# A planner's assumed distance from TensorE to its readers, its booking of indirect transfers, and its due times are changed

## The chip, the cores and the metric

The kernel runs on one core of one Trainium2 chip. The metric is the device time of one execution in microseconds; runs are compared by their median.

## The reference

Two parts, one after the other. The first is a causal convolution of 8 sequences of 5696 steps with 128 channels by a filter as long as the sequence, written with Fourier transforms. The second sends each of the 8 x 5696 = 45,568 rows of 128 numbers to one of eight experts.

```python
Yf = np.fft.rfft(x, n=2*S, axis=1) * np.fft.rfft(h, n=2*S, axis=0)[None]
x  = np.fft.irfft(Yf, n=2*S, axis=1)[:, :S, :].reshape(N, D)
logits = x @ w_gate + modality_bias[modality_id]
e_idx  = np.argmax(logits, axis=1)
gate_w = softmax(logits)[np.arange(N), e_idx]
for e in range(E):                                    # E = 8, F = 1024
    out[e_idx == e] = gate_w * (np.maximum(x @ w1[e], 0) @ w2[e])
```

## The kernel before, in words

All data are 32-bit floats. Where TensorE has to keep full precision at its fast rate, an operand is split into a high and a low part, and three products (high by high, low by high, high by low) stand for one. ScalarE makes the high part, VectorE or GpSimd the low one.

The eight sequences are worked in four groups of two (g = 0 to 3). For each group there are three passes: **first** (`stage1`, line 300, 45 columns in 23 pairs), which writes `z` to memory; **over** (`stage23`, 64 rows, lines 584 to 616), which multiplies by the filter's transform, transforms back in part and writes `u`; and **route** (`stage4`, 23 pairs in chunks of four), which ends the transform (line 700 or 706), turns the rows (line 718), makes the gate logits (line 725), ranks them on VectorE (lines 758 to 800), and sends each block of 128 rows to its expert's region with one indirect transfer on GpSimd's queue (line 814). A full chunk has 16 of these.

The experts' tiles follow: 81 of 512 rows and 23 of 256 in five **levels** of 14, 22, 22, 23 and 23. Level g needs the routed rows of groups 0 to g; the last two need all of them. A tile is loaded on SP's queue (line 895), with weights (line 902), turned (line 921), and then runs eight times: first product (lines 935 to 937), ReLU and high part on ScalarE (line 940), low part on VectorE (line 943), second product (lines 951 to 953). The result is copied, turned (line 960), weighted (line 963) and scattered with four indirect transfers (line 967).

Past the first pass of group 0 the order of each engine's instructions comes from `Plan`, an event simulation in Python that runs when the kernel is built. A step has a duration for each engine that may do it, steps that it waits for, buffers that it takes and gives back, and a due time. Whenever an engine is free in the simulation, it takes the ready step with the earliest due time. That order is all that is kept: on the chip each engine works through its list in that order and waits on semaphores; no planned time is executed. `SYNC` is the time that the plan leaves between the end of a step and the start of a step on another engine that reads it. `RATE` and `LAND` describe the one transfer channel of the plan: a load or store occupies it for its bytes by `RATE` and is there `LAND` later. Indirect transfers (steps with `lag`) don't occupy that channel; they are only kept to four in 5.6 us, or 6.8 us once the tiles' first due time is past. `AIMS` holds the due times at which each pass of each group and each level of tiles begins and ends; a pass's steps are spread evenly between them.

Buffers that tie the order: seven PSUM banks shared by all passes, three first products in flight (`ph_sl`), four pairs of `hh` and `hl`, six `t` buffers, one transfer list on SP.

Of the kernel before, what the change touches and what calls it, by code (L numbers as in the profile page):

```python
# [45 lines left out]
RTB = 8  # L46

AIMS = {
    "first": (None, (-302, 250), (72, 321), (497, 681)),
    "over": ((-196, 106), (75, 320), (458, 614), (745, 1009)),  # L50
    "route": ((65, 348), (139, 704), (632, 1015), (984, 1478)),
    "weights": (341, 635),
    "tiles": (405, 700, 1107, 1532, 1617, 1651),
}
RUNS = (1, 2, 2, 2, 4)
WP = 256
# [42 lines left out]
class Plan:  # L99

    SYNC = {"PE": 0.22, "DVE": 0.15, "ACT": 0.15, "POOL": 0.2, "SP": 0.1, "-": 0.0}
    LAND = 2.6
    RATE = 0.31e6
    BURST = 4, 5.6, 6.8

    def __init__(self):
# [17 lines left out]
    def run(self):  # L126
        ready = {e: [] for e in self.SYNC}
        busy = {e: False for e in ready}
        total = {e: 0.0 for e in ready}
        events = []  # L130
        count = 0
        channel = woken = 0.0
        begun = [-100.0] * self.BURST[0]

        def push(t, kind, x):
            nonlocal count
            heapq.heappush(events, (t, count, kind, x))
            count += 1

        def enable(x):  # L140
            if x.early is not None and now < x.due - x.early:
                push(x.due - x.early, "enable", x)
                return
            for e in x.work:
                bisect.insort(ready[e], (x.due, x.n, x))

        def release(steps):
            for y in steps:
                y.left -= 1
                if not y.left:  # L150
                    enable(y)

        def reached(x, same):
            e = next(iter(x.work))
            release(y for y in x.next if (list(y.work) == [e]) == same)

        def first(e):
            nonlocal woken

            apart = begun[-self.BURST[0]] + self.BURST[1 if now < AIMS["tiles"][0] else 2]  # L160
            kept = now >= apart and any(r[2].lag for r in ready["POOL"])
            for r in ready[e]:
                x = r[2]

                main = next(iter(x.work))
                if main != e and not (busy[main] or main == "POOL" and kept) or e == "POOL" and kept and len(x.work) > 1:
                    continue
                if x.lag and now < apart:
                    if woken < apart:
                        woken = apart  # L170
                        push(apart, "wake", None)
                    continue
                if all(len(p.idle) >= sum(q is p for q, _ in x.take) for p, _ in x.take):
                    return x

        now, started = 0.0, 0
        for x in self.steps:
            if not x.left:
                enable(x)
        while True:  # L180
            for e in ready:
                x = None if busy[e] else first(e)
                if x is None:
                    continue
                x.start = now
                started += 1
                for p, key in x.take:
                    x.st[key] = p.take()
                for o in x.work:
                    ready[o].remove((x.due, x.n, x))  # L190
                x.emit(e)
                busy[e] = True
                total[e] += x.work[e]
                end = now + x.work[e]
                push(end, "idle", (e, x))
                if x.lag:
                    begun.append(now)
                if x.bytes:
                    channel = max(channel, end) + x.bytes / self.RATE
                    end = channel + self.LAND  # L200
                    push(end, "same", x)
                else:
                    push(end if len(x.work) == 1 else end + self.SYNC[e], "same", x)
                push(end + x.lag, "done", x)
                push(end + x.lag + self.SYNC[e], "next", x)
            if not events:
                break
            now = events[0][0]
            while events and events[0][0] <= now:
                _, _, kind, x = heapq.heappop(events)  # L210
                if kind == "idle":
                    busy[x[0]] = False
                    release(x[1].behind)
                elif kind == "done":
                    for p, key in x.free:
                        p.give(x.st[key])
                elif kind == "enable":
                    x.early = None
                    enable(x)
                elif kind != "wake":  # L220
                    reached(x, kind == "same")
        assert started == len(self.steps), "steps that wait for each other"
        self.total, self.end = total, now
# [924 lines left out]
```

## Time and profile before

| | |
|---|---|
| median of 3 runs | 2410.16 us (2404.16 to 2418.43) |
| the profiled execution | 2395.75 us |
| its span, first to last instruction | 2394.0 us |
| TensorE busy | 2126.2 us (89%) |
| VectorE, ScalarE, GpSimd busy | 68%, 54%, 52% |
| mean granted TensorE clock | 0.932 |

A share is an average over passes with different limits, so the stretches are read one by one. "Waited for" is idle time of an engine in front of an instruction that ended when the named instruction was done; "issue" and "remote" are such time that the trace puts down to no instruction of the core. A busy TensorE counts modelled ends of its matmuls.

### The profile page before, as it was taken

What the parts mean: (1) busy time and instruction counts of PE and PEld (TensorE: products, weight loads), DVE (VectorE), ACT (ScalarE), POOL (GpSimd) and SP (SyncE); (2) the same over time, 40 slices, a digit from 0 to 9 for tenths busy, and PEclk for the clock granted to TensorE, in tenths of its full rate; (3) what the DMA queues carried; (4) which work ended last, traced back from release to release, by engine and by line L of the source; (5) the groups of instructions that cost most, each with busy time, mean ns of one, the idle gap of its engine ahead of it and who ended that gap; (6) DMA issues with size and microseconds to landing.
All of it is one profiled execution on the core that took longest, in us unless ns stands there. A gap on an engine that the chain in (4) does not pass through costs nothing.

```text
span 2394.0 us, 39278 instructions
## 1 busy us (share of the span) xinstructions
PE 2126.2 (89%) x11514; PEld 1774.0 (74%) x11514; DVE 1633.3 (68%) x3107; ACT 1291.1 (54%) x2584; POOL 1251.1 (52%) x1278
## 2 busy tenths in 40 slices
PE   5699876987999999788999999879878999999997
PEld 4577776765788787676888787658666778888897
DVE  5499764887689999776688986446434745555554
ACT  5566664654656676654556555335433444444453
POOL 2178554785477777567366665452444333333332
PEclk8899876998999999889999999889989999999999
DMA  8999765998998898764455643333212151122630
GB/s 285 301 298 299 246 215 172 289 329 275 280 304 282 275 312 266 243 226 135 118 151 165 196 125 121 123 116 92 84 55 93 45 151 44 45 80 69 222 107 26
DMA packets 228265, 434.54 MB, mean 182 GB/s; under 512 B 35798, under 2 KB 94906, under 8 KB 224209
## 3 DMA queue, kind: packets, MB, share of 16 engines
q1 hardware_dynamic: 204448, 384.15, 51.3%
q0 software_dynamic: 23600, 47.88, 6.1%
q8 instruction: 91, 1.49, 0.3%
q14 instruction: 126, 1.02, 0.1%
HBM read 408.11 MB, written 175.95 MB: 244 GB/s over the span
## 4 chain that ended last, share of the span: by engine, by line
PE 43%; issue 6%; DVE 5%; another core or an unknown queue 3%; DMA 2%; ACT 1%; POOL 1%; SPq 0%; POOLq 0%; DVEq 0%; ACTq 0%
PE bank L937 5%; PE bank L952 5%; PE bank L935 5%; PE bank L951 5%; PE bank L936 5%; PE bank L953 5%; PE bank L706 2%; PE bank L584 2%; PE pl L725 1%; PE bank L960 1%; PE bank L921 1%; DVE hl L943 1%; DVE t L591 1%; POOL out L967 1%
## 5 line engine op out<-in xcount | busy, mean ns | idle before, releaser
L943 DVE SCALAR_TENSOR_TENSOR hl<-bank,hh 128x512 fp32r<-128x512 f32 x740 | 503.7, 688 | 394.2 <-ACT hh L940 318.3
L940 ACT ACTIVATE hh<-bank 128x512 fp32r<-128x512 f32 x740 | 439.0, 598 | 524.3 <-PE bank L937 382.2
L967 POOL DMA_INDIRECT out<-of,mrt x370 | 370.2, 1001 | 514.5 <-DVE of L963 391.2
L814 POOL DMA_INDIRECT rows<-rt,idx x360 | 376.5, 1046 | 126.6 <-issue 94.2
L951 PE MATMUL bank<-hh,slot 128*128 128x512 f32 (+1 forms) x744 | 311.0, 418 | 46.5 <-ACT hh L940 32.3
L952 PE MATMUL bank<-hl,slot 128*128 128x512 f32 (+1 forms) x744 | 294.0, 395 | 17.2 <-DVE hl L943 11.7
L935 PE MATMUL bank<-mxh,slot 128*128 128x512 f32 (+1 forms) x744 | 305.4, 410 | 3.0 <-DMA slot<-weights 2.2
L936 PE MATMUL bank<-mxl,slot 128*128 128x512 f32 (+1 forms) x744 | 289.3, 389 | 4.0 <-DVE mxl L927 3.9
L953 PE MATMUL bank<-hh,slot 128*128 128x512 f32 (+1 forms) x744 | 289.7, 389 | 0.0
L591 DVE TENSOR_TENSOR t<-bank,hs 96x512 f32<-96x512 f32 x415 | 263.1, 677 | 38.3 <-PE bank L584 20.5
L937 PE MATMUL bank<-mxh,slot 128*128 128x512 f32 (+1 forms) x744 | 288.5, 388 | 0.0
L584 PE MATMUL bank<-zb,m 96*96 96x256 f32 x896 | 233.6, 390 | 2.8 <-DMA zb<-z 1.6
L951 PEld LDWEIGHTS bank<-hh,slot 128*128 128x128 f32 x744 | 144.5, 194 | 79.5 <-ACT hh L940 41.1
L952 PEld LDWEIGHTS bank<-hl,slot 128*128 128x128 f32 x744 | 144.4, 194 | 53.3 <-DVE hl L943 23.8
L584 PEld LDWEIGHTS bank<-zb,m 96*96 96x96 f32 x896 | 146.1, 168 | 46.3 <-DMA zb<-z 2.3
L401 ACT COPY ut<-bank 90x512 f32<-90x512 f32 x189 | 109.6, 581 | 108.5 <-PE bank L616 48.3
L937 PEld LDWEIGHTS bank<-mxh,slot 128*128 128x128 f32 x744 | 143.7, 193 | 29.6
L935 PEld LDWEIGHTS bank<-mxh,slot 128*128 128x128 f32 x744 | 144.1, 194 | 29.1 <-DMA slot<-weights 2.7
L936 PEld LDWEIGHTS bank<-mxl,slot 128*128 128x128 f32 x744 | 144.4, 194 | 28.3 <-DVE mxl L927 5.6
L953 PEld LDWEIGHTS bank<-hh,slot 128*128 128x128 f32 x744 | 144.0, 194 | 27.2
L300 PE MATMUL bank<-xx,ft 128*128 128x256 f32 x810 | 128.2, 311 | 20.7 <-ACT ft L504 20.5
L692 POOL TENSOR_TENSOR uu<-uu 128x512 fp32r<-128x512 f32 x48 | 62.4, 1308 | 148.6 <-ACT uu L688 147.2
(222 smaller groups left out, 4423.7 us busy)
## 6 DMA issues: line engine op xcount, KB each, us to landing
slot<-weights SPq DMA_DIRECT2D x158, 1024.0 KB
z<-z SPq DMA_DIRECT2D x180, 256.0 KB
uu<-u SPq DMA_DIRECT2D x159, 256.0 KB
zb<-z SPq DMA_DIRECT2D x112, 360.0 KB
u<-ut SPq DMA_DIRECT2D x112, 360.0 KB
raw<-in_w SPq DMA_DIRECT2D x88, 256.0 KB
mrt<-rows SPq DMA_DIRECT2D x81, 260.0 KB
hs<-hd SPq DMA_DIRECT2D x96, 192.0 KB
```

Of the source, the lines that this page charges most:

```text
L584: nc.tensor.matmul(two(st["px"])[:KP, h], mm, both["zb"][:, k % 2, 1 - h], start=True, stop=True)
L591: nc.vector.tensor_tensor(st[f"t{h}"].rearrange("p j (b d) -> p j b d", d=D), px[:KP, h].rearrange("p (b d) -> p b d", d=D).unsqueeze(1).t ...
L814: nc.gpsimd.indirect_dma_start(views[count[0] % NVIEW], bass.IndirectOffsetOnAxis(ap=rs["idx"][:, t + c:t + c + 1], axis=0), st["rt"][:, c ...
L935: nc.tensor.matmul(po, w[0][:, fs], xh, start=True, stop=False)
L936: nc.tensor.matmul(po, w[0][:, fs], xl, start=False, stop=False)
L937: nc.tensor.matmul(po, w[1][:, fs], xh, start=False, stop=True)
L940: nc.scalar.activation(hf["hh"], hf["ph"], AF.Relu)
L943: nc.vector.scalar_tensor_tensor(hf["hl"], hf["ph"], 0.0, hf["hh"].bitcast(F32), op0=ALU.max, op1=ALU.subtract)
L951: nc.tensor.matmul(po, w[0][:, fs], hf["hh"][:, cs], start=k == 0, stop=False)
L952: nc.tensor.matmul(po, w[0][:, fs], hf["hl"][:, cs], start=False, stop=False)
L953: nc.tensor.matmul(po, w[1][:, fs], hf["hh"][:, cs], start=False, stop=k == 7)
L967: nc.gpsimd.indirect_dma_start(oviews[(t * NSUB + c) % NVIEW], bass.IndirectOffsetOnAxis(ap=st["rt"].bitcast(I32)[:, c, D + 1:D + 2], axis=0),
```

## The change

Four things, all in what the plan assumes; no instruction of the kernel is written differently.

- `SYNC["PE"]`, the distance from the end of a TensorE step to steps of other engines that read it, goes from 0.22 to 1.5 us.
- Each indirect transfer books 66e3 bytes on the plan's transfer channel.
- `RATE` goes from 0.31e6 to 0.30e6 bytes a microsecond.
- The due times of all passes and levels are other ones.

```diff
 AIMS = {
-    "first": (None, (-302, 250), (72, 321), (497, 681)),
-    "over": ((-196, 106), (75, 320), (458, 614), (745, 1009)),
-    "route": ((65, 348), (139, 704), (632, 1015), (984, 1478)),
-    "weights": (341, 635),
-    "tiles": (405, 700, 1107, 1532, 1617, 1651),
+    "first": (None, (-356, 245), (71, 322), (490, 734)),
+    "over": ((-251, 93), (112, 389), (452, 612), (756, 1007)),
+    "route": ((113, 343), (138, 685), (612, 1003), (965, 1563)),
+    "weights": (343, 669),
+    "tiles": (392, 685, 1115, 1550, 1570, 1652),
 }
...
-    SYNC = {"PE": 0.22, "DVE": 0.15, "ACT": 0.15, "POOL": 0.2, "SP": 0.1, "-": 0.0}
+    SYNC = {"PE": 1.5, "DVE": 0.15, "ACT": 0.15, "POOL": 0.2, "SP": 0.1, "-": 0.0}
     LAND = 2.6
-    RATE = 0.31e6
+    RATE = 0.30e6
+    ROWS = 66e3
...
                 if x.lag:
                     begun.append(now)
+                    channel = max(channel, now) + self.ROWS / self.RATE
                 if x.bytes:
                     channel = max(channel, end) + x.bytes / self.RATE
```

## Rows read from the trace of the kernel before

**Rows 1.** The head of the page: span, and each engine's busy time, share and instructions; and the part on transfer queues, the queue of GpSimd's indirect transfers (packets, MB, share of the 16 transfer engines).

```profile
span 2394.0 us, 39278 instructions
PE 2126.2 (89%) x11514; PEld 1774.0 (74%) x11514; DVE 1633.3 (68%) x3107; ACT 1291.1 (54%) x2584; POOL 1251.1 (52%) x1278
...
q0 software_dynamic: 23600, 47.88, 6.1%
```

**Rows 2.** Busy time by stretch: the stretch and its length, then busy us (instructions) of TensorE, its weight loads, VectorE, ScalarE, GpSimd, then granted TensorE clock, share of the transfer engines, GB/s.

```profile
112.00:270.00 158.00, 149.88 (x880) 123.40 (x879) 151.97 (x231) 105.92 (x208) 120.87 (x116) 0.98 0.90 286
270.00:420.00 150.00, 108.53 (x627) 99.68 (x626) 83.16 (x190) 84.07 (x194) 69.91 (x66) 0.72 0.65 205
420.00:600.00 180.00, 154.97 (x790) 120.25 (x789) 149.62 (x314) 94.22 (x203) 122.75 (x131) 0.90 0.94 297
600.00:960.00 360.00, 341.09 (x1947) 284.57 (x1947) 318.59 (x565) 240.60 (x519) 248.28 (x250) 1.00 0.91 286
960.00:1140.00 180.00, 149.57 (x790) 123.88 (x788) 123.19 (x273) 102.83 (x215) 113.71 (x111) 0.89 0.63 199
...
1440.00:1960.00 520.00, 441.16 (x2104) 352.57 (x2103) 263.98 (x619) 224.58 (x438) 230.18 (x235) 0.90 0.32 97
1960.00:2394.00 434.00, 417.84 (x2469) 364.94 (x2468) 234.53 (x366) 203.65 (x365) 136.96 (x141) 0.99 0.26 87
```

**Rows 3.** TensorE's waits from 270 to 420 us, longest in total first: who waited for whom, us in total, times, longest.

```profile
PE bank L718 <- DVE rt L403: 16.0, 6, 11.9
PE pl L725 <- issue: 8.0, 4, 6.1
PE bank L718 <- issue: 6.8, 3, 3.2
PE bank L300 <- ACT ft L504: 5.6, 2, 2.8
...
```

**Rows 4.** The same from 420 to 600 us.

```profile
PE bank L610 <- issue: 6.2, 1, 6.2
PE bank L610 <- POOL t L598: 5.8, 8, 1.6
PE bank L610 <- DVE t L598: 3.0, 2, 2.8
...
```

**Rows 5.** The same from 960 to 1140 us.

```profile
PE bank L300 <- ACT ft L504: 10.8, 1, 10.8
PE bank L951 <- ACT hh L940: 9.9, 4, 3.8
PE bank L952 <- DVE hl L943: 3.2, 4, 2.4
PE bank L706 <- POOL uu L692: 3.1, 1, 3.1
...
```

**Rows 6.** The same from 1440 to 1960 us.

```profile
PE bank L951 <- ACT hh L940: 21.2, 7, 10.3
PE bank L951 <- issue: 13.9, 6, 6.6
PE bank L960 <- ACT ot L401: 10.1, 5, 4.2
PE pl L725 <- DVE yt L403: 6.1, 3, 3.4
PE bank L706 <- DVE hl L943: 5.1, 1, 5.1
PE bank L960 <- issue: 5.0, 2, 4.0
PE pl L768 <- DVE oh L763: 4.7, 2, 2.7
PE bank L936 <- DVE mxl L927: 3.9, 2, 3.7
PE bank L952 <- DVE of L963: 3.1, 1, 3.1
...
```

**Rows 7.** Instructions in order of time, three steps of a tile in the last stretch: start, duration, engine, line, operation, and in brackets the engine's idle time before it and what ended it.

```profile
2002.64 0.39 PE L937 MATMUL bank<-mxh,slot 128*128 128x512 f32 x1
2003.07 0.60 ACT L940 ACTIVATE hh<-bank 128x512 fp32r<-128x512 f32 x1 [0.80 <-PE bank L937]
2003.69 0.69 DVE L943 SCALAR_TENSOR_TENSOR hl<-bank,hh 128x512 fp32r<-128x512 f32 x1 [0.71 <-ACT hh L940]
```

**Rows 8.** Instructions in order of time around 1600 us: the first and the last of GpSimd's 20 transfers that follow one another there, then ScalarE's and SP's next instructions.

```profile
1587.49 1.00 POOL L814 DMA_INDIRECT rows<-rt,idx  x1 [2.11 <-DVE rt L800]
...
1611.81 0.97 POOL L967 DMA_INDIRECT out<-of,mrt  x1 [0.30 <-issue]
1615.73 1.08 ACT L940 ACTIVATE hh<-bank 128x512 fp32r<-128x512 f32 x2 [13.33 <-remote]
1615.73 0.08 SPq L902 DMA_DIRECT2D slot<-weights  x1
```

**Rows 9.** Instructions in order of time at the end of the last route pass: its last logits, the first transfer of its last chunk, and the first load of a tile of the fourth level.

```profile
1860.28 0.51 PE L725 MATMUL pl<-wg,yt 128*128 128x8 f32 x4
1910.22 0.99 POOL L814 DMA_INDIRECT rows<-rt,idx  x1 [7.98 <-DVE rt L800]
1948.09 0.36 SPq L895 DMA_DIRECT2D mrt<-rows  x1
```

## The prediction, made before the changed kernel ran

> **What bounds the kernel now.** I read the head of the page first: TensorE is busy 2126 of 2394 us, no other engine above 68% [rows 1]. So the question is where TensorE is not kept busy. Busy time by stretch answers it [rows 2]. From 112 to 270 us and from 600 to 960 us VectorE is the fuller engine or nearly so (152 of 158, 319 of 360 us) and TensorE misses only 8 and 19 us. From 1960 us to the end only tiles are left; TensorE misses 16 of 434 us and has its clock. The loss lies in four stretches: 270 to 420 (108.5 of 150 us busy, granted clock 0.72), 420 to 600 (155 of 180, 0.90), 960 to 1140 (150 of 180, 0.89) and 1440 to 1960 (441 of 520, 0.90). In the first, third and last of them no engine is full, so there the order of the lists sets the pace.
>
> TensorE's waits in these stretches say what it stands behind [rows 3 to 6]: nearly always a reader of its own results (rt, hh, hl, ot, yt, t) on ScalarE, VectorE or GpSimd, or time put down to nobody. A transfer is not among the long ones. The timeline of one of the longest shows a second thing [rows 8]: GpSimd issues 20 indirect transfers without a pause from 1587.5 to 1612.8 us, and ScalarE and SP both stand until 1615.73 us, 3 us after the last one ends; ScalarE had stood for 13.3 us, with TensorE's product done. A wait like this has no producer that could be ordered earlier.
>
> **The change, part by part.** Nothing is added or removed; the 39,278 instructions stay, but for low parts that the plan may hand from VectorE to GpSimd or back. What can change is each engine's order, SP's transfer list and GpSimd's included.
>
> *The distance, 0.22 to 1.5 us.* In the trace ScalarE starts 0.43 us after the last of three matmuls starts, and VectorE's part begins 0.62 us after that [rows 7]; 0.22 is therefore about the true distance, and 1.5 is slack, 1.28 us of it. Each reader of TensorE, and all that follows from it, TensorE's own next step included, is planned 1.28 us later, so some 1.28 us more of independent matmuls stand ahead of every matmul that needs a reader. A wait on a reader can shrink by at most 1.28 us. From the rows, taking min(longest, 1.28) for the longest of each row and at most 1.28 us for each of the others: [rows 3] 5.4 + 3.2 + 3.8 + 2.6 = 15.0 of 36.4 us; [rows 4] 1.3 + 5.8 + 1.5 = 8.6 of 15.0; [rows 5] 1.3 + 5.1 + 2.1 + 1.3 = 9.8 of 27.0; [rows 6] 9.0 + 7.7 + 6.4 + 3.8 + 1.3 + 2.3 + 2.6 + 1.5 + 1.3 = 35.9 of 73.1. The sum is 69 of 152 us. That is the upper bound by this part alone. The lower bound is nothing: at most three first products may be in flight, so in a burst like [rows 8] the extra work is used up at the first wait, and the later waits of the same burst end when GpSimd ends. I take half, 35 us, because in the last stretch the 7 waits of one row include one of 10.3 us and six that share 10.9 us [rows 6]: the short ones can go, the long ones can't. In the stretches where VectorE is full I take nothing; a deeper order can't speed VectorE.
>
> In the last stretch I take nothing either: its order already lets TensorE run (418 of 434 us).
>
> *The clock.* A stretch with waits has a granted clock of 0.72 to 0.90 and one without has 0.98 to 1.00 [rows 2]; that is a mixture of 1.2 and 2.4 GHz, and each wait that goes also gives some of it back. The Trainium skill, page "TensorE: Matmul & The Clock Gate", section "Why this matters for your kernels", says that idle gaps between bursts of matmuls put the clock back to its lower level; the trace agrees (0.72 where the waits are thickest). By it the gain would exceed the waits. I leave this gain out of the sum and let it stand against waits that arise anew.
>
> *The booking and the rate.* An indirect transfer moves 47.88 MB / 730 = 66 KB [rows 1], so the booking is true to size: 0.22 us of channel each, 160 us over the kernel, and every load behind it is planned that much later. Where transfers are dense (0.90 to 0.94 of the engines [rows 2]) work that reads a load then stands later in the lists of ScalarE and VectorE, which could only help; but TensorE shows no long wait on a load there. The lower end is nothing. The upper end is the one wait that ends with a load's conversion, 10.8 us at ft [rows 5], which the first term has already counted by 1.3. I take nothing.
>
> *The due times.* For most passes they move by under 40 us and keep their order. One pair moves against another: the last route pass (984 to 1478, now 965 to 1563) against the third level's tiles (1107 to 1532, now 1115 to 1550). Its last pair was due at 984 + 494 x 22/23 = 1456.5 and is now due at 1537. Tiles due behind it: (1532 - 1456.5)/19.3 = 3.9 before, (1550 - 1537)/19.8 = 0.7 now. These tiles hide the chain from the last logits to the fourth level. It took from 1860.3 to 1948.1 us [rows 9], 88 us, but 50 us of that pass before the last chunk's first transfer, which in the end waited for VectorE's line 800. Ranking is a few short instructions; if 40 of the 50 us can go, 48 are needed, and cover that shrinks by 3.2 tiles of 434/34.5 = 12.6 us (23 tiles and 23 half ones [rows 2]), 40 us, just about still hides it. The range of this part is 0 to +40 us; I take 0. On the other side the same work is spread over 598 instead of 494 us, so chunks of 16 transfers stand further apart; I count no gain for it, since a chunk's 16 still become ready together.
>
> Sum: 2395.75 us for the profiled execution, less 35, is 2361. That execution lay 14.4 us under the median of the runs (2410.16). On the scale of the median I predict **2375 us**; with one fifth to all of the bound, its own range is 2341 to 2396.
>
> **The rivals.**
>
> *The bursts decide, and the time stays.* TensorE's long waits end when GpSimd's run of transfers ends [rows 8], the 16 transfers of a chunk become ready at once in either plan, and the distance is no part of that. Then 2410, give or take 12. For it: of the 152 us, 83 lie beyond the 1.28. Against it: many short waits that are plainly readers, such as the eight at t of 5.8 us [rows 4].
>
> *A hole before the fourth level; slower.* The cover of the last route pass is gone and VectorE still makes the tables first. TensorE then stands 40 us at the change of level; the last stretch of gain is lost and of the other three half remains (17 us): 2395.75 - 17 + 40 + 14.4 = 2433. It decides if the last chunk's first transfer (line 814) starts less than about 38 us before the third level's last matmul (from its 1910.2 to the load at 1948.1 it was 38 us [rows 9]). For it, the arithmetic of the due times; against it, the slack that the chain has.
>
> *Buffers run short in the plan; slower.* A bank is held 1.28 us longer at every step: the plan counts 0.88 + 0.22 + 1.30 = 2.40 us for line 584 and its reader, then 3.68. If seven banks don't do, the plan starts steps late and the order in the full stretches has holes that the chip does not need. If VectorE in 600 to 960 us fell to its share of 420 to 600 (0.83 instead of 0.885), that stretch would take 23 us more, and with no gain elsewhere the time is 2433 too. The Trainium skill speaks for this rival: "PSUM — Partial Sum Buffer", section "Summary: rules for kernel authors", asks to empty PSUM promptly because it is tight. The rows before show no sign of it, but they are of the short distance.
>
> *The bursts break up; faster than forecast.* With readers later, more low parts wait for GpSimd between transfers, and a run of 20 falls into shorter ones. Then the rows' waits in 1440 to 1960 go (73) with the bounds of the other three (33): 2395.75 - 106 + 14.4 = 2304. For it, the wider route pass; against it, VectorE is half empty there (264 of 520 us [rows 2]), so it will keep most low parts.
>
> **How the numbers follow.** Forecast 0.46, no change 0.20, hole 0.14, short buffers 0.08, broken bursts 0.12. This kernel's runs spread over 0.6%, so 0.5%, 12 us, is about what can be told from no change. Faster by more: most of the forecast and the broken bursts, 0.57; within: 0.21; slower: 0.22. The range 2318 to 2431 leaves out about two thirds of the broken bursts and half of either slower case, 0.19 in all.
>
> **What would show it.** Right: fewer and shorter waits of lines 951, 960, 718 and 610 on their readers in the four stretches, with the waits of over 5 us still there at runs of 16 to 20 transfers; the last 434 us unchanged; the clock in the second stretch above 0.72. Wrong: a gap of TensorE over 10 us where the first tile of the fourth level is loaded (hole); VectorE's share from 600 to 960 us under 0.85 (buffers); no run of over 12 transfers past 1440 us (bursts broken); or gains in the stretches where VectorE is full, which I price at nothing.

## The result

| | before | after |
|---|---|---|
| median of 4 runs, us | 2407.16 (2397.46 to 2418.43) | 2291.59 (2286.97 to 2298.12) |
| profiled execution, us | 2395.75 | 2289.67 |
| its span, us, and mean granted clock | 2394.0, 0.932 | 2287.8, 0.953 |

The ratio of the medians is 0.952 (0.947 to 0.957). The kernel is 116 us faster; 35 were forecast, and 2291.59 lies under the range. The direction is right and the size is not. Lines of the kernel after stand two lower than those of before: 935 is now 937, 940 is 942, 960 is 962.

Four runs of those below took 680 to 2910 us longer than the others of their kernel; the ratios leave them out, the medians do not.

The head of the page after answers to [rows 1]. TensorE's modelled busy time fell by 50 us (2126 to 2076) and its idle time by 55 (211 to 156, counted from the instructions in order of time, from the first matmul past the first pass of group 0, at 111 and 108 us, to the last matmul).

```profile
span 2287.8 us, 39250 instructions
...
PE 2076.3 (91%) x11514; PEld 1751.0 (77%) x11514; DVE 1637.0 (72%) x3097; ACT 1276.0 (56%) x2579; POOL 1256.2 (55%) x1293
```

Busy time by stretch, kernel after, columns as in [rows 2]; the last stretch starts with its fourth level:

```profile
270.00:420.00 150.00, 114.81 (x717) 105.39 (x716) 98.71 (x216) 91.58 (x215) 86.83 (x85) 0.78 0.76 241
420.00:600.00 180.00, 148.82 (x744) 115.48 (x743) 144.05 (x286) 90.80 (x195) 118.57 (x131) 0.91 0.91 281
600.00:960.00 360.00, 346.88 (x2001) 294.48 (x1999) 320.49 (x602) 242.53 (x526) 254.60 (x253) 0.99 0.91 286
960.00:1140.00 180.00, 158.51 (x869) 133.21 (x870) 133.16 (x264) 103.20 (x221) 112.04 (x111) 0.94 0.63 199
...
1844.00:2287.00 443.00, 425.21 (x2494) 370.57 (x2492) 233.38 (x369) 205.46 (x369) 138.30 (x143) 0.99 0.27 87
```

Equal clock times are no longer equal work, so I compare where each level begins. The first products of the first four levels start at 599.6, 1075.6, 1546.09 and 1957.17 us before, and at 560.7, 1031.4, 1503.71 and 1843.99 us after; the fifth level follows the fourth. The kernel after is 39 us ahead at the first level, 44 at the second, 42 at the third and 113 at the fourth; what follows takes 437 us before and 444 after.

Even these places are not equal work. Counted in order of time, 2562, 5052, 7381 and 9034 matmuls stand ahead of the four levels before, and 2446, 4971, 7441 and 9021 after. The first level is 39 us earlier with 116 fewer matmuls ahead of it, so a part of the 39 is work put off. The idle time of TensorE has no such doubt: up to the first level, in each of the first three levels, and behind them it is 75, 38, 31, 64 and 4 us before, and 72, 30, 26, 23 and 6 after. So 41 of the 55 us went within the third level. That level's own stretch, first in the kernel before and then in the kernel after:

```profile
1546.09:1957.17 411.08, 347.52 (x1654) 278.02 (x1653) 204.77 (x466) 173.32 (x335) 180.43 (x184) 0.91 0.31 91
```

```profile
1503.71:1843.99 340.28, 317.21 (x1581) 258.73 (x1580) 198.15 (x448) 161.72 (x312) 179.44 (x185) 0.97 0.34 106
```

TensorE's waits there, kernel after, longest first; they answer to [rows 6]:

```profile
PE bank L962 <- ACT ot L403: 8.6, 4, 3.1
PE bank L953 <- issue: 6.4, 1, 6.4
PE bank L923 <- DMA mrt<-rows: 2.8, 1, 2.8
PE bank L953 <- ACT hh L942: 1.7, 2, 1.5
```

The wait of the second product on ScalarE's ReLU, 21.2 us with one of 10.3 in [rows 6], is 1.7 us, from 1440 us on too. Between 1440 and 1503.71 us one longer wait stands, 8.9 us at line 962, put to "issue". The 10.3 us wait was one that ends with GpSimd's run of transfers, the sort that I had said would stay; in the kernel before, in order of time, right behind ScalarE's row of [rows 8]:

```profile
1616.38 0.80 PE L951 MATMUL bank<-hh,slot 128*128 128x512 f32 x1 [10.32 <-ACT hh L940]
```

ScalarE's own waits tell the same. These are its longest rows put to "remote" over the whole execution, first in the kernel before, then in the kernel after; "remote" means here that the trace shows nothing on the core that ended them:

```profile
ACT hh L940 <- remote: 58.4, 15, 13.3
...
ACT gt L676 <- remote: 15.3, 1, 15.3
...
ACT ot L401 <- remote: 9.6, 3, 6.5
```

```profile
ACT ot L403 <- remote: 12.8, 2, 11.3
...
ACT yt L403 <- remote: 10.7, 2, 8.8
...
ACT hh L942 <- remote: 9.3, 4, 3.2
```

All such waits of ScalarE come to 103 us before and 56 after. Before, each of the 26 ends inside a run of eight or more transfers or less than 5 us behind one. VectorE has such waits too, 42 us before and 20 after. The longest wait of [rows 3], 11.9 us of line 718 for VectorE, was of this sort as well: in the kernel before, ScalarE and VectorE were released together, 2.6 us after a run of 20 transfers had ended at 392.86 us:

```profile
395.48 0.40 ACT L676 CAST gt<-gs 128x256 fp32r<-128x256 f32 x1 [15.34 <-remote]
395.53 0.69 DVE L403 COPY rt<-bank 128x512 f32<-128x512 f32 x1 [13.12 <-remote]
```

SP's list stands with them (kernel before, then after):

```profile
SPq L902 <- remote: 72.2, 6, 25.6
```

```profile
SPq L669 <- remote: 14.9, 3, 9.5
```

### The profile page after: what moved, and what is told of

Its sections match the earlier page's. It is cut to its first block, busy times and chain, and to the rows that moved or that the text cites. A ratio compares the mean times of both kernels' runs of the same rounds, so it can differ in the third digit from the quotient of the medians.

```text
span 2287.8 us, 39250 instructions
## 1 busy us (share of the span) xinstructions
PE 2076.3 (91%) x11514; PEld 1751.0 (77%) x11514; DVE 1637.0 (72%) x3097; ACT 1276.0 (56%) x2579; POOL 1256.2 (55%) x1293
## 5 line engine op out<-in xcount | busy, mean ns | idle before, releaser
L953 PE MATMUL bank<-hh,slot 128*128 128x512 f32 (+1 forms) x744 | 306.0, 411 | 9.6 <-issue 6.4
L954 PE MATMUL bank<-hl,slot 128*128 128x512 f32 (+1 forms) x744 | 287.1, 386 | 4.3 <-DVE hl L945 3.2
L955 PE MATMUL bank<-hh,slot 128*128 128x512 f32 (+1 forms) x744 | 285.3, 384 | 0.0
L599 POOL TENSOR_TENSOR t<-t,t 96x256 f32<-96x256 f32 x88 | 71.6, 813 | 140.3 <-DVE t L593 104.3
```

What stands on the lines that cost most here:

```text
L953: nc.tensor.matmul(po, w[0][:, fs], hf["hh"][:, cs], start=k == 0, stop=False)
L954: nc.tensor.matmul(po, w[0][:, fs], hf["hl"][:, cs], start=False, stop=False)
L955: nc.tensor.matmul(po, w[1][:, fs], hf["hh"][:, cs], start=False, stop=k == 7)
```

## The experiments

My theory after the result had two parts. The distance removes waits on readers, as forecast, and it also shortens what ScalarE and SP stand while GpSimd's transfers run without a pause [rows 8]. The first rival: the new due times and the booking do the second part, by spreading the chunks. The second rival: the standing has no price, and all of the gain is order.

A fact for reading what follows: the runs are of several chips, and the chips are of two kinds. On chips 0 and 5 and on the one of the result above, whose number is not known, the kernel before takes 2391 to 2407 us. On chips 8, 12 and 7 it takes 2232 to 2233 us, and in no trace taken there is a wait of ScalarE or VectorE put to "remote". I call the first kind **standing**, because there engines stand in runs of transfers, and the second **quiet**. The unaltered kernel before was timed on the quiet chips but not traced there. Each numbered chip was used for one set of runs, so whether a chip keeps its kind is not shown. Each ratio is against the kernel before on the same chip.

### The parts, on a quiet chip (chip 8, before 2232.38 us)

*The distance alone:*

```diff
-    SYNC = {"PE": 0.22, ...
+    SYNC = {"PE": 1.5, ...
```

> The kernel before with one part of the change: the distance from TensorE to its readers 1.5 instead of 0.22 us; due times, rate and booking as before. If the distance is what gained (theory one: short waits on readers go, and with them the lower clock), most of the 116 us come with it: 2300 to 2345 us. If the due times are what gained (theory two: the last route pass is spread wider and the runs of transfers fall apart), this stays within 2395 to 2425. If the parts only work together (theory three: due times are set for one plan and are wrong for another), it is 2360 to 2450, without a side.

2212.58 us, 0.991 (0.987 to 0.995).

*The due times alone:*

```diff
-    "first": (None, (-302, 250), (72, 321), (497, 681)),
...
+    "tiles": (392, 685, 1115, 1550, 1570, 1652),
```

> The kernel before with the new due times alone; distance 0.22, rate and booking as before. Theory one (distance): 2390 to 2425. Theory two (due times): 2300 to 2345, with no run of over 12 transfers past 1440 us. Theory three (together): above 2390, perhaps slower than before, up to 2460.

2300.64 us, 1.029 (1.025 to 1.034), slower. TensorE's waits, longest first:

```profile
PE bank L922 <- DMA mrt<-rows: 29.3, 2, 27.9
PE bank L611 <- POOL t L599: 19.0, 9, 9.4
PE ps L301 <- ACT xx L318: 15.2, 10, 3.4
```

The 27.9 us are the hole before the fourth level that the prediction has as a rival. They are less than half of the 68 us lost; the rest was not followed.

*The booking and the rate alone:*

```diff
-    RATE = 0.31e6
+    RATE = 0.30e6
+    ROWS = 66e3
...
+                    channel = max(channel, now) + self.ROWS / self.RATE
```

> The kernel before with the booking of indirect transfers and the rate of 0.30e6 alone; distance 0.22 and due times as before. Theories one and two: 2395 to 2420, no change that can be told. If the booking is what gained (readers of loads were planned too early where transfers are dense), 2300 to 2350, and the gain lies between 270 and 1140 us.

2274.32 us, 1.019 (1.016 to 1.022), slower. Its trace has a run of 20 transfers without a pause too. First that run in the kernel before on its standing chip [rows 8], then here:

```profile
1587.50:1616.50 29.00, 14.61 (x65) 10.68 (x64) 6.88 (x12) 5.55 (x11) 19.49 (x20) 0.79 0.30 97
```

```profile
1481.80:1511.30 29.50, 29.50 (x155) 24.70 (x153) 15.68 (x25) 16.38 (x31) 19.89 (x21) 1.00 0.61 212
```

GpSimd does the same in both (20 and 21 instructions, 19.5 and 19.9 us). On the quiet chip TensorE is busy for all of it at full clock and the transfers move 212 GB/s; on the standing chip TensorE is busy for half of it, at a granted clock of 0.79, and 97 GB/s are moved. So a run of transfers does not stop the other engines everywhere, and a run of 20 is not by itself the cause. These two kernels differ in order; one and the same kernel on both kinds of chip follows under chip 5.

*All but the distance*, the kernel after with

```diff
-    SYNC = {"PE": 1.5, ...
+    SYNC = {"PE": 0.22, ...
```

> The changed kernel with the distance set back to 0.22 us, all else as changed. Theory one: 2370 to 2420, nearly all of the gain is gone. Theory two: 2290 to 2310. Theory three: over 2400.

2289.99 us, 1.025 (1.020 to 1.030), slower, with a hole of 28.3 us before the fourth level.

### The parts, on standing chips

On chip 0 (before 2391.31 us) the kernels of both sides were run again.

> The changed kernel itself, unaltered, beside the kernel before on whatever chip this call gets, since the kernel before took 2232 us on the chip of the last call and 2407 on the first. If the change gains by waits that only the first chip has (ScalarE and SP standing through runs of indirect transfers), then on a chip where the kernel before takes about 2232 us this takes 2200 to 2250, within 1% of it. If the gain is of the order of the lists and holds on any chip, it is 4 to 5.5% under the kernel before: 2110 to 2145 beside 2232, or 2275 to 2310 beside 2407.

2298.41 us, 0.961 (0.957 to 0.966).

> The kernel before, unaltered, for its profile beside the one above. On a chip like that of the last call: 2225 to 2240 us, TensorE without any wait of over 2 us inside a run of 16 or more indirect transfers, and its first product of the fourth level about 150 us earlier than 1957 us. On a chip like the first: 2395 to 2420 and the same waits as shown.

2394.78 us in the one run taken; 125 of its 217 us of idle TensorE lie in runs of eight or more transfers, as in the first trace (122 of 211).

*The kernel after without the booking:*

```diff
-    RATE = 0.30e6
+    RATE = 0.31e6
...
-                    channel = max(channel, now) + self.ROWS / self.RATE
```

> The changed kernel without the booking of indirect transfers and with the rate back at 0.31e6; distance 1.5 and due times as changed. If the booking carries little (the prediction's view), within 1% of the changed kernel run beside it. If the due times were found for the plan with the booking and lose their sense without it, 1.5 to 4% over it.

2335.47 us, 0.974 (0.969 to 0.980): 37 us worse than with it, and the intervals lie apart.

*The kernel after with the due times of before:*

```diff
-    "first": (None, (-356, 245), (71, 322), (490, 734)),
...
+    "tiles": (405, 700, 1107, 1532, 1617, 1651),
```

> The changed kernel with the due times of the kernel before; distance 1.5 and booking as changed. If the due times carry the gain (the last route pass spread over 598 instead of 494 us), 2% or more over the changed kernel run beside it. If the distance carries it, within 1.5% of it.

2315.23 us, 0.966 (0.962 to 0.970). That is 17 us over the whole change, but the two intervals overlap. With the longer distance and the booking the new due times cost nothing, and may win some of the 17 us.

On chip 5 (before 2406.07 us) two of the kernels of chip 8 were run again, *all but the distance* and *the distance alone*.

> Again the changed kernel with the distance back at 0.22 us. On the chip where the kernel before took 2232 us this took 2290. On a chip where the kernel before takes about 2395 and the changed one 2298: if the distance carries the gain, 2370 to 2470; if due times and booking carry it there by shorter runs of transfers, 2300 to 2340.

2449.68 us, 1.017 (1.011 to 1.023), slower. TensorE's waits from 1950 to 2020 us, longest first, and the two ends of the chain behind the longest in the order of time:

```profile
PE bank L923 <- DMA mrt<-rows: 27.3, 1, 27.3
```

```profile
1953.17 0.51 PE L727 MATMUL pl<-wg,yt 128*128 128x8 f32 x4
...
2004.37 1.11 PE L923 MATMUL bank<-ident,mrt 128*128 128x128 f32 x4 [27.31 <-DMA mrt<-rows]
```

> Again the kernel before with the distance of 1.5 us alone. It took 2212 beside 2232 us on the one chip. On a chip where the kernel before takes about 2395: if the distance carries the gain by itself, 2295 to 2330; if the distance needs the booking and the new due times to show, 2350 to 2400.

2323.75 us, 0.964 (0.960 to 0.968). The same edit that won 20 us on a quiet chip wins 82 here.

This kernel is the same one on both chips, so a run of 20 transfers can be compared with itself. It starts at 1546.25 us on the standing chip 5 and at 1479.89 us on the quiet chip 8, and its transfers take 25.7 us on both:

```profile
1546.20:1576.00 29.80, 19.50 (x81) 14.40 (x80) 7.65 (x12) 7.56 (x15) 19.95 (x20) 0.80 0.19 56
```

```profile
1479.80:1509.60 29.80, 29.80 (x152) 24.84 (x151) 15.23 (x24) 14.61 (x27) 22.90 (x23) 1.00 0.49 151
```

TensorE is idle for 10.3 us of it on the one and for none on the other. So with every engine's order the same, this run costs something on the one chip and nothing on the other.

The first rival fails here: the distance alone, with the due times and the booking of before, wins 82 us, and the due times and the booking without the distance win nothing (2449.68 us).

### The runs of transfers by themselves, on the standing chip 5

The kernel before, in its own order, with GpSimd given something else to do after every fourth transfer of an unbroken run: five short memsets of a tile that nobody reads. The order of TensorE, ScalarE and VectorE is that of the kernel before in the trace too, instruction by instruction.

```diff
+                if e == "POOL":
+                    self.run4 = self.run4 + 1 if x.lag else self.run4 if x.work[e] < 0.5 else 0
+                    if x.lag and self.run4 % 4 == 0:
+                        self.space()
...
+    pause = cp.tile([128, 120], F32, name="pause")
+    plan.space = lambda: [nc.gpsimd.memset(pause, 0.0) for _ in range(5)]
```

> The kernel before with five short memsets on GpSimd (some 1 us together) after every fourth indirect transfer that follows another without a longer GpSimd step between; the plan does not know of them, so all other lists are unchanged. If runs of transfers without a pause make ScalarE and SP stand, 50 to 110 us are saved on a chip where the kernel before takes about 2395, and the waits of over 5 us that ended 3 us after a run are gone. If the waits have another cause, or the pause is too short to matter, the time is that of the kernel before or up to 20 us more. On a chip like that with 2232 us, within 0 to +20 us of the kernel before in either case.

2283.17 us, 0.947 (0.943 to 0.951): as much as the whole change won, and more than the 50 to 110 us expected. That is against the second rival, since no engine but GpSimd has another order. How GpSimd's list looks now, in order of time:

```profile
1569.47 0.97 POOL L974 DMA_INDIRECT out<-of,mrt  x1 [0.30 <-issue]
1570.43 1.24 POOL L338 MEMSET pause<- 128x120 f32 x5
1572.30 0.97 POOL L974 DMA_INDIRECT out<-of,mrt  x1 [0.63 <-issue]
```

No wait of ScalarE or VectorE is put to "remote" any more, and none of SP's. The stretch from 1440 us to about the fourth level (1840.8 us), where TensorE had been busy for 441 of 520 us at 0.90 [rows 2]:

```profile
1440.00:1847.00 407.00, 393.51 (x2017) 325.88 (x2016) 248.01 (x552) 214.69 (x417) 273.44 (x481) 0.97 0.37 119
```

The same pauses in the kernel after:

> The changed kernel with the same memsets. If the runs are what costs, it is 30 to 65 us under the changed kernel on a chip where that takes 2298 (2230 to 2270), a version that beats both; if not, 2295 to 2320. On a chip where the kernel before takes 2232 us there is nothing to save; it then stands near what the changed kernel does there, 2170 to 2230 by the first theory.

2284.74 us, 0.948 (0.944 to 0.952), between the two ranges expected. With the runs broken, the change is worth nothing more on a standing chip. The table is counted from the instructions in order of time, in us. Idle TensorE is split into what lies in runs and what lies outside; a run is at least eight transfers with pauses under 0.8 us between them, and is taken to end 4 us after its last. "Lower clock" is 2 x (1 - mean granted clock) x span, the time at 1.2 GHz if the rest is at 2.4:

```
kernel                 chip   span    PE busy  idle  in runs  outside  lower clock  ScalarE "remote"
before                 first  2394.0  2126     211   122      89       326          103
after                  first  2287.8  2076     156   72       84       215          56
after                  0      2294.2  2078     162   74       88       225          74
distance alone         5      2336.5  2103     178   89       89       276          86
after, no booking      0      2337.5  2106     177   72       104      257          53
after, old due times   0      2318.7  2092     171   85       86       255          93
after, short distance  5      2451.6  2133     263   135      129      363          108
before, paused         5      2281.0  2085     139   0        139      205          0
after, paused          5      2281.3  2084     143   0        143      224          2
```

### On quiet chips again

Chip 12 (before 2232.09 us): the distance with pauses, the kernel after unaltered, the kernel before with a pause after every eighth transfer only (`% 8`), and a distance of 3.0.

> The kernel before with the distance of 1.5 us and with the pauses (five memsets after every fourth transfer of a run); due times, rate and booking as before. With pauses alone it was 2283. If the distance gains only by what ScalarE's standing in runs costs, 2275 to 2295. If it has a gain of its own on waits outside the runs (20 us, as 2212 against 2232 on the chip without such standing), 2245 to 2268, faster than the changed kernel by 1 to 2%. On the chip without standing: 2205 to 2235.

2257.40 us, 1.011 (1.009 to 1.012), over the 2205 to 2235 expected. The distance without pauses was 0.991, so pauses after every fourth cost some 45 us (2257 here against 2213 on chip 8) where there is nothing to win. If they cost as much on a standing chip, the paused kernels' 2283 us would be near 2240 without that cost, which is about what the kernel before takes on a quiet chip; this is an estimate, no run shows it.

> The changed kernel unaltered, as the reference of this call. Beside a kernel before of about 2395 to 2407: 2290 to 2300, ScalarE's waits put down to nobody 55 to 75 us. Beside a kernel before of about 2232, where ScalarE does not stand: 2190 to 2215 if the due times cost nothing once the distance is there, 2215 to 2260 if they cost.

2207.54 us, 0.988 (0.984 to 0.992). The whole change wins 25 us on a quiet chip. Here the stretch before the fourth level has no idle TensorE at all:

```profile
1440.00:1780.00 340.00, 340.00 (x1771) 283.84 (x1770) 221.63 (x486) 184.29 (x350) 197.45 (x204) 1.00 0.41 128
```

> The kernel before with the same pause after every eighth transfer of a run instead of every fourth. If only runs of 12 and more cost (in the kernel before the runs of 8 had 0 to 3.4 us of TensorE's idle time each, the ones of 20 had 13 to 18), it keeps most of the gain: 2270 to 2300. If runs of 8 cost as much for each transfer, half the gain is left: 2325 to 2355.

2233.72 us, 1.002 (1.000 to 1.003). Pauses after every eighth cost next to nothing.

> The kernel before with a distance of 3.0 us, twice that of the change; due times, rate and booking as before. If slack acts through more work ahead of TensorE, another 10 to 40 us against 1.5 us (2285 to 2315). If three first products and four pairs of hh and hl are all that can be ahead, no more than at 1.5 us: 2315 to 2345. If the plan runs out of banks or buffers, over 2345.

2250.25 us, 1.008 (1.007 to 1.010), slower: 3.0 is too far. Busy time from 600 to 960 us, first with a distance of 1.5, then with 3.0:

```profile
600.00:960.00 360.00, 346.94 (x1980) 294.62 (x1979) 315.56 (x600) 244.21 (x535) 255.45 (x250) 0.98 0.91 290
```

```profile
600.00:960.00 360.00, 339.56 (x1929) 284.65 (x1928) 301.37 (x558) 232.02 (x506) 250.14 (x247) 0.99 0.87 276
```

VectorE, the fuller engine of this stretch, falls from 0.877 to 0.837 of it. That is what the rival of the short buffers expects; that the buffers are what runs short was not tried.

The last two runs were meant to show pauses after every eighth transfer on a standing chip, but they are of the quiet chip 7 (before 2233.24 us).

> The changed kernel with five short memsets after every eighth transfer of a run. Beside a kernel before of about 2395 to 2407: if a run has to pass eight before anything stands and the rarer pause costs next to nothing, 2225 to 2265, better than the changed kernel (2298) and than pauses after four (2285); if not, 2275 to 2300. Beside a kernel before of about 2232: 2200 to 2220, as the changed kernel.

2216.59 us, 0.992 (0.990 to 0.994).

> The kernel before with the pause after every eighth transfer. It took 2234 beside 2232 where nothing stands. Beside a kernel before of about 2395 to 2407: 2270 to 2300 if only runs of 12 and more cost; 2325 to 2355 if runs of 8 cost as much for each transfer.

2236.20 us, 1.002 (1.000 to 1.004). So whether a pause after every eighth transfer is enough on a standing chip stays open.

## Why the prediction was wrong in size

**The step that failed: "the short ones can go, the long ones can't", with its ground, "A wait like this has no producer that could be ordered earlier".** I took the waits at runs of transfers as fixed, because the distance does not act on them one by one. They were the larger part of what could be won. TensorE's idle time within runs went from 122 to 72 us, outside them from 89 to 84. That these runs cost what they do is shown by the kernel before with pauses: with the other engines' orders untouched and 900 memsets added it is 123 us faster. That most of the gain hangs on the standing is shown by the two kinds of chip: the whole change wins 25 us where nothing stands and 93 to 116 where something does. It also fits that the change wins nothing beside the pauses, though these have a price of their own.

How the change shortens the standing is only partly seen. There are fewer long runs (98 transfers in runs of 16 or more before, 40 after; distance alone 72), and each transfer of a run of eight or more costs less (idle TensorE 122/242 = 0.50 us before, 72/215 = 0.33 after, 89/219 = 0.41 with the distance alone). The second fits the longer reserve: in the third level, the median number of matmuls between a first product and the second product that reads it is 12 before and 19 after. But it is 19 with the distance alone too, so the reserve is not all of it. No run separates the two.

**The distance, 35 us.** On a quiet chip it is measured by itself: 2232.38 to 2212.58, 20 us, inside the 0 to 69 of the bounds and under the half that I took. That leaves the rule of at most 1.28 us for each wait standing, but no run tested it wait by wait. The places came out otherwise. Half the bound of [rows 3, 4] is 12 us, and the idle time up to the first level fell by 2; half of [rows 5] is 5, and in the first two levels the idle time fell by 14; half of [rows 6] is 18, and in the third level it fell by 41, most of that in runs of transfers (54 to 22 us). One sum of the prediction is off by a little: by its own rule 5.8 in [rows 4] is 5.5, and the 69 stays.

**The clock, left out of the sum.** This was the other failing term. The time at the lower clock fell from 326 to 215 us, and the modelled busy time fell by 50 us with the same number of matmuls (11,514), nearly as much as the idle time (55). I let it stand against new waits; there were few. The Trainium skill, "TensorE: Matmul & The Clock Gate", section "Why this matters for your kernels", has gaps between bursts of matmuls put the clock back to its lower level; the traces agree, and the paired lines of the third level show it at 0.91 with 63.6 us idle and at 0.97 with 23.1.

**The booking and the rate, "I take nothing".** Wrong, and of both signs. Alone they lose 1.9% on a quiet chip; with the distance and the new due times their absence costs 37 us on a standing one, with 104 us idle outside runs against 88 on the same chip. Which of the orders does it was not followed.

**The due times, 0 with a range to +40.** Here cover means the tiles of the third level that are left to hide the chain from the last logits to the fourth level. The arithmetic was right in kind where the distance is short: holes of 27.9, 28.3 and 27.3 us. In the last of these the chain took 2004.37 - 1953.17 = 51 us from the last logits to the first turn; I had 48. With the distance of 1.5 there is no hole, and the last logits come 89 us before the fourth level's first product:

```profile
1755.25 0.51 PE L727 MATMUL pl<-wg,yt 128*128 128x8 f32 x4
...
1843.99 0.40 PE L937 MATMUL bank<-mxh,slot 128*128 128x512 f32 x1
```

Before it was 1957.17 - 1860.28 = 97 us [rows 9]. That one edit opens the hole and another closes it was in no term: I worked the due times out by themselves, with the order of the short distance. Why the longer distance brings the last logits forward against the tiles was not followed further.

**Right.** The stretch where VectorE is full gained little (TensorE busy 341.09 us from 600 to 960 before, 346.88 after) and the last stretch nothing (437 and 444 us). Of the rivals, "The bursts break up" (2304) lies nearest to what came, and was held at 0.12. Its sign was too strict: past 1440 us the runs of 12 and more went from 16, 20, 12, 20 and 14 transfers to 16 and 13, so they grew fewer and shorter and did not vanish. "The bursts decide" was right that they decide, and wrong that the time stays.

## What to carry to other kernels

When several engines stand at once and are released at once behind another engine's unbroken run of work, treat the run as a cost that can be broken up, and price it by an experiment that only breaks it; don't take it for fixed because no producer is late. When idle gaps go, count the clock that comes back beside them: here the busy time fell by nearly as much as the idle time. Where work is reordered, the time at which a pass begins is no measure until the work ahead of it is counted. Edits of a planner are judged together and on one chip: due times that lose 2.9% by themselves, and a booking that loses 1.9%, did no harm with the longer distance.

## What the runs showed that I had not expected

- The same kernel takes 2391 to 2407 us on some chips and 2232 to 2233 us on three others, 7% apart. On the slower ones ScalarE, VectorE and SP's list stand in long runs of indirect transfers [rows 8], 103, 42 and 72 us in the first trace; on the others no trace shows it, not even for the same run of 20 in the same kernel. Neither what differs in the chips nor what holds the engines was found; shown is only that breaking the run ends it.
- About 1.24 us of other work on GpSimd after every fourth transfer removes all of it, and makes the kernel before 123 us faster on such a chip; the same pauses cost some 45 us with the distance of 1.5 on a quiet one.
- A distance of 1.5 us, where the chip needs about 0.2 to 0.6 [rows 7], is better than the true one on both kinds, and 3.0 is worse than either on a quiet chip (2250 against 2213 and 2232 us).
- No kernel tried beats the changed one on both kinds of chip: the paused ones take 2283 and 2285 us on a standing chip, against 2298 and 2292 for the changed kernel on two others, and the changed kernel has the best time on a quiet chip, 2207.54 us.
